# Scores by even and odd query blocks over three PSUM banks, weighted sums in four 64 by 64 tiles, from the third batch on

## The chip, the cores and the metric

The kernel runs on one NeuronCore of a Trainium2 chip. The metric is the device time of one execution in microseconds (us). Three runs of the kernel before gave 892.37, 891.59 and 891.19 us.

## The reference

Masked attention of 8 batches, 8 heads, 576 positions and 64 dimensions feeds a two-layer network with a softplus.

```python
scores = scale * np.matmul(q, k.transpose(0, 1, 3, 2))
mask_local = (rel >= 0) & (rel < stride)
mask_strided = (rel >= 0) & (pos[None, :] % stride == pos[:, None] % stride)
masks = np.stack([mask_local if h < H // 2 else mask_strided for h in range(H)], axis=0)
scores = np.where(masks[None, :, :, :], scores, -1000000000.0)
...
attn = attn / (np.sum(attn, axis=-1, keepdims=True) + 1e-09)
return np.matmul(attn, v).astype(np.float32)
...
h = x @ w_in
g = np.maximum(h, 0.0) + np.log1p(np.exp(-np.abs(h)))
return (g @ w_out).astype(np.float32)
```

The stride is 32, `x` is the attention's output as 4608 tokens of 512, and the layers are 512 by 2048 and 2048 by 512. Four heads look at the last 32 positions (local), four at the positions of their own class modulo 32 (strided). After the host has put the strided heads' positions in the order of their classes, in both kinds a block of 32 queries needs only its own 32 keys and the 32 keys ahead of them.

## The kernel before

**Two heads are a pair**: head 0 lies on partitions 0 to 63 and head 1 on 64 to 127. There are 8 batches times 4 pairs, numbered n = 0 to 31, a local and a strided pair in turn. A pair has 18 blocks of 32 queries, 9 in each half (`place`) of the sequence.

**Scores** of a pair (`score_steps`, L306, matmul in L343) are 36 small matmuls: 18 blocks times two heads, each with 64 rows (dimensions), 32 stationary columns (queries) and 64 moving columns (keys). Operands are fp32, which the chip works off in two passes, so the trace has two rows for each. The 9 blocks of a half are cut into two parts (`SPLIT`): six go to the bank `ps`, three to the upper part of the bank `po`. The two heads take different row halves of the array, and the halves of the sequence and the heads take different column quarters; part 0 takes four of the eight 64 by 32 tiles, and part 1 (`place_of`) the other four. `zip_longest` in `scores` (L353) deals the matmuls of the two parts in turn, as long as both have some.

**Between scores and sums** VectorE adds the mask on the way out of PSUM (`add_mask`, L409; tasks Y), takes maxima, subtracts, sums and normalizes; ScalarE does the exponential; VectorE transposes the weights in blocks of 32 by 32 into `pt` (L451, tasks P).

**Weighted sums** (`weighted`, L502, matmul in L519) use spans of 96 queries: 6 spans times 2 heads are 12 matmuls of 128 rows (the span's 96 keys and the 32 ahead), 64 stationary columns (the values) and 96 moving columns. The two heads are two 128 by 64 tiles. The three spans of half 0 go to the lower part of `po`, those of half 1 to a bank of the pool `ps_h`, named `pv`. From there ScalarE and VectorE make the high and the low part of x (`x_part`, L557 and L555; tasks H and L).

**The network** takes x in chunks of 512 tokens: 16 steps f for each of 9 chunks. A step is `hidden` (L623, tasks F: 12 matmuls of 128 by 128 by 512 into a bank of `ps_h`), the softplus on ScalarE (L635, L638, L640) and VectorE (L644, tasks u), its high and low part (L253 `gh`, L656 `gl`), and two steps later `output` (L663, tasks O: 12 matmuls of the same size into the four banks `py`).

**PSUM has eight banks**: `ps`, `po`, two of `ps_h`, four `py`. The two of `ps_h` are dealt in turn to the steps F and, between them, to `pv`.

**The order of the work** is written out by hand (`FIRST`, L36) up to the first steps of chunk 1; from there the class `Plan` (L80) places tasks with given costs, due times and predecessors on the engines, and the instructions are issued in the order of its start times. From batch 2 on (n = 8 to 31) the scores of pair n and the sums of pair n-1 are one task S{n} on TensorE (L863), placed between an F and an O. The step F after it waits for `L{n-1}1` (L814), the low part of x that is the last reader of `pv`. Pair 8 has no sums ahead of it, and the sums of pair 31 are a task by themselves (L895), so there are 23 such joint tasks.

Of the kernel before, what the change touches and what calls it, by code (L numbers as in the profile page):

```python
# [19 lines left out]
P = 128  # L20
# [99 lines left out]
def attention_softplus_ffn(  # L120
# [32 lines left out]
    st_pool = ctx.enter_context(tc.tile_pool(name="st", bufs=4))  # L153
    u_pool = ctx.enter_context(tc.tile_pool(name="u", bufs=2))
    io_pool = ctx.enter_context(tc.tile_pool(name="io", bufs=4))
    ps_s = ctx.enter_context(tc.tile_pool(name="ps_s", bufs=1, space=bass.MemoryType.PSUM))
    ps_o = ctx.enter_context(tc.tile_pool(name="ps_o", bufs=1, space=bass.MemoryType.PSUM))
    ps_h = ctx.enter_context(tc.tile_pool(name="ps_h", bufs=2, space=bass.MemoryType.PSUM))
# [35 lines left out]

    prob_early = [early["l", pair][:, PAD + S :] for pair in PAIRS[:-1]] + [prob_all]
    prob_early = [t[:, : PAD + 3 * PAD * NCHK] for t in prob_early]
    py = [ps_y.tile([P, DM], F32, name=f"py{t}") for t in range(TPC)]
    ident_b = const.tile([P, P], BF16, name="ident_b")

# [12 lines left out]
    vs, pss, sts, pos, shared = ({} for _ in range(5))  # L212
    taken = []
    phs, us, ghs, gls = {}, {}, {}, {}

    def is_local(n):
        return order[n][1] < NPAIR // 2
# [46 lines left out]
    def load_v(n):  # L264
        b, pair = order[n]
        if n < NPAIR:

            t = room[n]
        else:
            t = v_in  # L270
        t = t[:, : 2 * NTILE * D].rearrange("p (a c) -> p a c", c=2 * D)
        src = v[b, pair]
        nc.sync.dma_start(t[PAD:P, 0], src[0:TILE])  # L273
# [17 lines left out]
    for t in room + [v_in]:  # L291
        nc.gpsimd.memset(t[0:PAD, : 2 * D], 0.0)
# [13 lines left out]
    def score_steps(n, part):  # L306
# [43 lines left out]
        if masked and n == 0:  # L350
            add(False)

    def scores(n, parts=range(2)):  # L353

        for _ in zip_longest(*[score_steps(n, part) for part in parts]):
            pass

    def parts(n, part=None):
        if n not in sts:
            sts[n] = st_pool.tile([P, 4, NCHK], F32, tag="stat", name=f"st_{n}")  # L360
        lo, hi = (0, NCHK) if part is None else SPLIT[part]
# [76 lines left out]
    def normalize(n, engine):  # L438
        pv, _, (_, _, _, rc) = parts(n)
        engine.tensor_tensor(pv, pv, rc.unsqueeze(2).broadcast_to(pv.shape), op=ALU.mult)  # L440

    def prob_transposes(n, quarters=range(4)):
        p = prob_of(n)
        for quarter in quarters:
# [54 lines left out]
        dst = pt_of(n, 2 * g)  # L499
        copy_on(engine, dst, src)  # L500

    def weighted(n, half, joint=False):  # L502


        if joint:
            if half == 0:
                po = shared[n + 1]
            else:
                po = ps_h.tile([P, 512], F32, tag="ph", name=f"pv_{n}")
        elif half == 1 and (n == NPAIR - 1 or n >= 2 * NPAIR):  # L510
            taken.append(n)
            po = ps_s.tile([P, 512], F32, tag="ps", name=f"pv_{n}_{half}")
        else:
            po = ps_o.tile([P, 512], F32, tag="po", name=f"pv_{n}_{half}")
        pos[n, half] = po
        for x in range(NTILE // 2):
            a = NTILE // 2 * half + x
            for h in range(2):
                nc.tensor.matmul(  # L519
                    po[64 * h : 64 * h + 64, TILE * x : TILE * x + TILE],  # L520
                    lhsT=vs[n][:, a, h, :],
                    rhs=pt_of(n, a)[:, h, a % 2],
                    start=True,
                    stop=True,
                )
# [176 lines left out]

    first["mask"] = lambda: nc.scalar.dma_start(mask_b, masks)
    first["W"] = lambda: dummies(10)
    for n in range(2 * NPAIR + 2):
# [83 lines left out]
    def joint(i):  # L789
        return pair_at.get(i, 0) > 2 * NPAIR  # L790
# [4 lines left out]
    for i in range(NFC, len(steps) + 8):  # L795
        when[i] = t
        if i >= begin:
            w = CH[steps[min(i, len(steps) - 1)][0]] / 384
            t += 4.2 * w + (1.3 if i in pair_at else 0) + (1.3 if joint(i) else 0)
    plan = Plan()  # L800
    add = plan.add
    wanted = {}
# [5 lines left out]
    for i in range(begin, len(steps) + LAG):  # L808
        if i < len(steps):
            c, f = steps[i]  # L810
            w, x = CH[c] / 384, when[i]
            after = [f"F{i-1}", f"u{i-2}"] + wanted.get(c, [])
            if joint(i - 1):
                after.append(f"L{pair_at[i - 1] - 1}1")  # L814
            add(f"F{i}", x, "PE", 2.1 * w, lambda c=c, f=f: hidden(c, f), after)
            after = [f"F{i}", f"l{i-2}"]
            add(f"A{i}", x + 2, "ACT", 1.5 * w, lambda c=c, f=f: log_part(c, f), after)
# [27 lines left out]
                fn = lambda c=c, t=t, engine=engine: result(c, t, engine)  # L845
                add(f"y{k}.{t}", x + 0.7 * t + 0.7, e, cost, fn, [name])
    def sums_of(n):
        for half in range(2):
            weighted(n, half, n != last)

    i_of = {n: i for i, n in pair_at.items()}
    for i, n in pair_at.items():
        x = when[i]
        if n > 2 * NPAIR:
            z = x - (when[i] - when[i - 2] if i - 2 in when else 0.0)
            add(f"Q{n}", z, "ACT", 2.5, lambda n=n: lay_out_q(n), [f"q{n}", f"S{n-1}"])
        after = [f"Q{n}", f"k{n}", f"Y{n-1}0", f"Y{n-1}1", f"L{n-2}1"]
        cost = 1.3
        if joint(i):
            cost = 2.5  # L860
            after += [f"P{n-1}", f"v{n-1}", f"u{i-1}"]

        def work(i=i, n=n):  # L863
            scores(n)
# [5 lines left out]
        for j in range(2):  # L870
            after = [f"S{n}", f"P{n-2}"]
            add(f"Y{n}{j}", y + j, "DVE", 0.47, lambda n=n, j=j: add_mask(n, j), after)
        after = [f"Y{n}0", f"Y{n}1"]
        for j, (letter, e, cost, fn) in enumerate(
            (
                ("x", "DVE", 0.75, row_maxima),
# [113 lines left out]
```

## Time and profile before

| What | Value |
|---|---|
| Median of three runs | 891.59 us |
| The profiled execution itself | 891.65 us |
| Span of its trace, first to last instruction | 889.8 us |
| TensorE (PE) busy | 880.2 us, 99% |
| VectorE (DVE) busy | 574.1 us, 65% |
| ScalarE (ACT) busy | 404.7 us, 45% |
| GpSimd (POOL) busy | 56.1 us, 6% |
| DMA, mean over the span | 66 GB/s |

A row of the timeline has the start in us from the span's start, the length in us, the engine, the line of the kernel, the operation, output and inputs, shapes, and how many instructions were merged (x12). PE is the matmul, PEld the load of its stationary operand. Matmuls overlap in their pipeline, so what one costs is read from the distance of two starts and not from its length. In brackets stands how long the engine was idle before, and what released it.

### The profile page before, as it was taken

The page shows a single profiled execution, that of the slowest core. Times are in us where ns is not written, and L with a number is a line of the kernel's source. Part 1 is how long each engine was busy: PE and PEld are TensorE (multiplying, and loading weights), DVE is VectorE, ACT ScalarE, POOL GpSimd, SP SyncE. Part 2 cuts the span into 40 slices and gives each one's busy share as a digit, 9 for nine tenths or more (in the row PEclk, how much of TensorE's full clock was granted, in tenths as well). Part 3 has the DMA queues.
Part 4 walks back from the last instruction along what each step waited for, and adds up shares of the span by engine and source line. Part 5 has one row for each costly group of instructions (what it writes and reads, how often), then busy time and mean ns, then how long its engine had stood idle before and what let it go on. Part 6 is the DMA issues. An engine that isn't in the chain of part 4 may idle for free.

```text
span 889.8 us, 16585 instructions
## 1 busy us (share of the span) xinstructions
PE 880.2 (99%) x6786; PEld 720.1 (81%) x6786; DVE 574.1 (65%) x1263; ACT 404.7 (45%) x764; POOL 56.1 (6%) x84
## 2 busy tenths in 40 slices
PE   8899999999999999999999999999999999999998
PEld 6777888888888888888888888888888888888886
DVE  5878876778766777776766676677777333333332
ACT  5898655354443344344444344334433333333332
POOL 3354340000000000000000000000000000000000
PEclk9999999999999999999999999999999999999999
DMA  9856212222211112111211121111200010001001
GB/s 338 289 200 242 76 34 75 59 60 60 88 32 31 45 54 82 45 31 45 91 45 45 44 92 30 30 43 54 82 18 18 1 48 1 0 1 48 1 1 47
DMA packets 50091, 58.41 MB, mean 66 GB/s; under 512 B 3168, under 2 KB 35296, under 8 KB 50016
## 3 DMA queue, kind: packets, MB, share of 16 engines
q1 hardware_dynamic: 49728, 57.03, 19.9%
q8 instruction: 53, 0.87, 0.4%
q10 hardware_dynamic: 288, 0.33, 0.1%
q14 instruction: 22, 0.18, 0.1%
HBM read 47.91 MB, written 9.44 MB: 64 GB/s over the span
## 4 chain that ended last, share of the span: by engine, by line
PE 96%; DMA 1%; SPq 1%; ACT 0%; DVE 0%; issue 0%; ACTq 0%
PE py L663 45%; PE ph L623 44%; PE ps L343 3%; PE pv L519 2%; PE po L519 2%; DMA early_l<-in_qk_dram 1%; DMA ri<-in_moe_w_in_dram 1%; PE po L343 0%; SPq L273 0%; SPq L262 0%; SPq L563 0%; PE ps L324 0%; SPq L280 0%; SPq L250 0%; PE pt L489 0%
## 5 line engine op out<-in xcount | busy, mean ns | idle before, releaser
L663 PE MATMUL py<-w_o,gh 128*128 128x512 f32 x1152 | 358.4, 392 | 0.0
L623 PE MATMUL ph<-x_h,w_i 128*128 128x512 f32 x1152 | 355.6, 390 | 0.0
L635 ACT ACTIVATE u<-ph 128x512 f32<-128x512 f32 x144 | 86.2, 599 | 399.8 <-PE ph L623 399.5
L623 PEld LDWEIGHTS ph<-x_h,w_i 128*128 128x128 f32 x1152 | 215.7, 188 | 45.3 <-issue 0.2
L663 PEld LDWEIGHTS py<-w_o,gh 128*128 128x128 f32 x1152 | 213.9, 188 | 46.6
L663 PE MATMUL py<-w_o,gl 128*128 128x512 f32 x576 | 224.4, 390 | 0.0
L623 PE MATMUL ph<-x_l,w_i 128*128 128x512 f32 x576 | 224.1, 389 | 0.0
L644 DVE SCALAR_TENSOR_TENSOR u<-ph,u 128x512 f32<-128x512 f32 x144 | 99.3, 690 | 173.2 <-ACT u L640 171.5
L451 DVE STREAM_TRANSPOSE pt<-prob 32x192 f32<-32x192 f32 x448 | 140.1, 317 | 6.8
L663 PEld LDWEIGHTS py<-w_o,gl 128*128 128x128 f32 x576 | 108.1, 188 | 22.8
L623 PEld LDWEIGHTS ph<-x_l,w_i 128*128 128x128 f32 x576 | 108.2, 188 | 22.6
L656 DVE TENSOR_TENSOR gl<-u,gh 128x512 fp32r<-128x512 f32 x136 | 94.3, 694 | 12.0 <-ACT gh L253 1.4
L638 ACT ACTIVATE u<-u 128x512 f32<-128x512 f32 x144 | 91.3, 634 | 4.4
L640 ACT ACTIVATE u<-u 128x512 f32<-128x512 f32 x144 | 91.1, 633 | 4.5
L253 DVE CAST gh<-u 128x512 fp32r<-128x512 f32 x128 | 54.5, 426 | 10.5 <-DVE u L644 0.5
L409 DVE TENSOR_TENSOR prob<-ps,mask_b 128x384 f32<-128x384 f32 x24 | 13.4, 558 | 51.4 <-PE ps L343 51.4
L253 ACT COPY qT<-prob 128x576 f32<-128x576 f32 x28 | 35.9, 1283 | 0.5 <-DMA prob<-in_qk_dram 0.5
L424 ACT ACTIVATE prob<-prob 128x576 f32<-128x576 f32 x24 | 16.5, 687 | 39.3 <-DVE prob L418 39.3
L343 PEld LDWEIGHTS ps<-kT,qT 64*32 64x32 f32 x1440 | 24.8, 106 | 9.7 <-issue 9.3
L343 PE MATMUL ps<-kT,qT 64*32 64x64 f32 x1440 | 30.0, 221 | 0.0
L555 DVE TENSOR_TENSOR x_l<-pv,x_h 128x288 fp32r<-128x288 f32 (+2 forms) x47 | 18.8, 413 | 10.1 <-ACT x_h L557 9.5
L557 ACT CAST x_h<-pv 128x288 fp32r<-128x288 f32 (+2 forms) x47 | 16.8, 375 | 12.6 <-PE pv L519 12.4
(94 smaller groups left out, 483.7 us busy)
## 6 DMA issues: line engine op xcount, KB each, us to landing
v_in<-in_v_dram SPq DMA_DIRECT2D x28, 320.0 KB, 3.5
out_dram<-o SPq DMA_DIRECT2D x35, 256.0 KB, 2.1
ri<-in_moe_w_in_dram SPq DMA_DIRECT2D x16, 512.0 KB, 6.4
ro<-in_moe_w_out_dram SPq DMA_DIRECT2D x16, 512.0 KB, 6.9
kT<-in_qk_dram SPq DMA_DIRECT2D x28, 288.0 KB, 3.3
prob<-in_qk_dram SPq DMA_DIRECT2D x28, 288.0 KB, 2.7
v_in<-in_v_dram SPq DMA_DIRECT2D x28, 48.0 KB, 3.1
room<-in_v_dram SPq DMA_DIRECT2D x4, 320.0 KB, 6.4
```

What stands on the lines that cost most here:

```text
L253: (engine.copy if engine is nc.scalar else engine.tensor_copy)(dst, src)
L343: nc.tensor.matmul(ps[to : to + 32, 64 * (x - lo) : 64 * (x - lo) + 64], lhsT=queries(n, head, c // 32), rhs=k_of(n)[head, c : c + 64], st ...
L451: nc.vector.transpose(pt[32 * (i + c) : 32 * (i + c) + 32, h, a : a + hi - lo, 32 * i : 32 * i + 32,], src[:, lo:hi, 32 * c : 32 * c + 32],)
L519: nc.tensor.matmul(po[64 * h : 64 * h + 64, TILE * x : TILE * x + TILE], lhsT=vs[n][:, a, h, :], rhs=pt_of(n, a)[:, h, a % 2], start=True, ...
L555: nc.vector.tensor_tensor(place("l"), cut(lo, hi), high, op=ALU.subtract)
L623: nc.tensor.matmul(ph, lhsT=w32["i", f][:, half, cc * P : (cc + 1) * P], rhs=x_of(x, cc)[:, t0 : t0 + n], start=(i == 0), stop=(i == 3 * N ...
L635: nc.scalar.activation(us[c, f], phs[c, f], AF.Abs)
L638: nc.scalar.activation(u, u, AF.Exp, scale=-1.0)
L640: nc.scalar.activation(u, u, AF.Ln, bias=1.0)
L644: nc.vector.scalar_tensor_tensor(u, in0=phs.pop((c, f)), scalar=0.0, in1=u, op0=ALU.max, op1=ALU.add)
L656: engine.tensor_tensor(g, us.pop((c, f)), ghs[c, f].bitcast(F32), op=ALU.subtract)
L663: nc.tensor.matmul(py[t], lhsT=g[:, sl], rhs=w32["o", f][:, half], start=(f == 0 and n == 0), stop=(f == NFC - 1 and n == 2),)
```

## The change

For n = 8 and above (`is_late`) three things are done in another way.

**Scores** (`late_scores`): the 9 blocks of a half are dealt by even (five) and odd (four). The even ones go to a bank of `ps_h` (columns 0 to 319), the first three odd ones to `ps` (columns 288 to 479), the fourth odd one to `po` (columns 288 to 351). The matmuls are of the same number and size; even and odd groups of four alternate, and the even blocks take the four tiles of the old part 0, the odd ones the other four. The mask is added in three instructions in place of two, of 320, 192 and 64 columns, with a second mask tile `mask_s` for strided pairs that is loaded by 10 DMAs (`Km`).

**Weighted sums** (`late_weighted`): the keys of a half are cut into five windows of 64. Half 0 lies on partitions 0 to 63 and half 1 on 64 to 127, so half and head make four tiles of 64 by 64. An even block has all its 64 keys in one window; an odd block has 32 in each of two windows, whose sums are added up in PSUM, the other halves of its weights being zeros that four GpSimd memsets write once (`Kz`). A window serves three blocks (96 moving columns), the first and the last two (64): 20 matmuls in place of 12, half 0 into `ps` and half 1 into `po`. The weights' transposes (`late_transposes`) are as many as before, with 160 and 128 columns in place of 192 and 96. The values come in three DMAs for each pair in place of two.

**The plan**: S costs 1.1 and 2.0 in place of 1.3 and 2.5, the times `when` follow, the F after S waits for `Y{n}0` (the mask of the even blocks) in place of `L{n-1}1`, and S waits for `u{i-1}` from n = 8 on.

```diff
+SPLIT_LATE = [(0, 5), (5, 8), (8, 9)]
...
-A15 L70 V71 H71 lo13 Bo14 do14 ho14 lo14 O13 Ae15 L71 v8 Al15 u15 Gh15 Q1 Gh14 Gl14 O14 Bo15
-do15 D8 Q0 QA1 Gl15 Qu1 QA0 Qu0 ho15 lo15 O15 Qh0 y0 Ob15 q9 y1 Qh1 Ql0 y2 y3 Ql1
+A15 L70 V71 Kz H71 lo13 Bo14 do14 ho14 lo14 O13 Ae15 L71 v8 Al15 u15 Gh15 Q1 Gh14 Gl14 O14 Bo15
+do15 D8 Q0 QA1 Gl15 Qu1 QA0 Qu0 ho15 lo15 O15 Qh0 y0 Ob15 q9 Km y1 Qh1 Ql0 y2 y3 Ql1
...
+        pss[n, 0] = ps_h.tile([P, 512], F32, tag="ph", name=f"ps_{n}_0")
+        for j in range(2):
+            pss[n, 1 + j] = shared[n][j][:, S // 2 :]
+        for x in range(5):
+            for part, j, block in ((1, x, 2 * x + 1), (0, x, 2 * x)):
+                if part == 1 and x == 4:
+                    continue
+                if part == 1 and x == 3:
+                    part, j = 2, 0
+                for place in range(2):
+                    c = 9 * 32 * place + 32 * block
+                    for h in range(2):
+                        to = 64 * place + 32 * (h if part == 0 else 1 - h)
...
+        for w in range(5):
+            lo, hi = max(2 * w - 1, 0), min(2 * w + 2, 9)
+            for half in range(2):
+                rows = slice(64 * half, 64 * half + 64)
+                for h in range(2):
+                    nc.tensor.matmul(
+                        banks[half][64 * h : 64 * h + 64, 32 * lo : 32 * hi],
+                        lhsT=vs[n][rows, w, h, :],
+                        rhs=pt_late[rows, h, w, 32 * (lo + 1 - 2 * w) : 32 * (hi + 1 - 2 * w)],
+                        start=w == 0,
+                        stop=w == 4,
...
-            if joint(i - 1):
-                after.append(f"L{pair_at[i - 1] - 1}1")
+            if i - 1 in pair_at:
+                after.append(f"Y{pair_at[i - 1]}0")
...
-        after = [f"Q{n}", f"k{n}", f"Y{n-1}0", f"Y{n-1}1", f"L{n-2}1"]
-        cost = 1.3
+        after = [f"Q{n}", f"k{n}", f"Y{n-1}1", f"Y{n-1}2", f"L{n-2}1"]
+        cost = 1.1
+        after.append(f"u{i-1}")
         if joint(i):
-            cost = 2.5
-            after += [f"P{n-1}", f"v{n-1}", f"u{i-1}"]
+            cost = 2.0
+            after += [f"P{n-1}", f"v{n-1}"]
```

**TensorE, the first joint task** (the scores of pair 9 with the sums of pair 8). Before; `ph` is the hidden step ahead of it, `ps_0` and `po` take the two parts of the scores, `pv` the sums of half 1:

```order
L623 MATMUL ph_5_2061<-x_l_666,w_i_905 128x512
L343 MATMUL ps_0_2080<-kT_101,qT 32x64 x4
L343 MATMUL po_2081<-kT_101,qT 32x64 x4
L343 MATMUL ps_0_2080<-kT_101,qT 32x64 x4
L343 MATMUL po_2081<-kT_101,qT 32x64 x4
L343 MATMUL ps_0_2080<-kT_101,qT 32x64 x4
L343 MATMUL po_2081<-kT_101,qT 32x64 x4
L343 MATMUL ps_0_2080<-kT_101,qT 32x64 x12
L519 MATMUL po_2081<-pt,v_in 64x96 x6
L519 MATMUL pv_2124<-pt,v_in 64x96 x6
L663 MATMUL py_104<-w_o_970,gh_3_2029 128x512 x2
```

And now; `ps_0` is the bank of `ps_h` with the even blocks, `ps` has odd blocks and half 0 of the sums, `po` the last odd block and half 1 of the sums:

```order
L428 MATMUL ps_2099<-kT_104,qT 32x64 x4
L428 MATMUL ps_0_2101<-kT_104,qT 32x64 x4
L428 MATMUL ps_2099<-kT_104,qT 32x64 x4
L428 MATMUL ps_0_2101<-kT_104,qT 32x64 x4
L428 MATMUL ps_2099<-kT_104,qT 32x64 x4
L428 MATMUL ps_0_2101<-kT_104,qT 32x64 x4
L428 MATMUL po_2100<-kT_104,qT 32x64 x4
L428 MATMUL ps_0_2101<-kT_104,qT 32x64 x8
L445 MATMUL ps_2099<-pt,v_in 64x64 x2
L445 MATMUL po_2100<-pt,v_in 64x64 x2
L445 MATMUL ps_2099<-pt,v_in 64x96 x2
L445 MATMUL po_2100<-pt,v_in 64x96 x2
```

Four more rows of 64x96 and two of 64x64 follow, in the same turn of `ps` and `po`, and then the same O as before. The groups of four score matmuls now alternate up to the last two, and the sums alternate between the banks in twos where one bank came after the other in sixes. The places of F, O and S against each other are the same in both programs from batch 2 on.

**VectorE after the same task.** Before; L409 adds the mask, L555 makes the low part of x, L414 takes the maxima:

```order
L409 TENSOR_TENSOR prob<-ps_0_2080,mask_b 128x384
L409 TENSOR_TENSOR prob<-po_2081,mask_b 128x192
L555 TENSOR_TENSOR x_l_376<-po_2081,x_h_362 128x288
L414 TENSOR_REDUCE st_2148<-prob 128x9
L555 TENSOR_TENSOR x_l_376<-pv_2124,x_h_362 128x96
L555 TENSOR_TENSOR x_l_376<-pv_2124,x_h_362 128x192
```

And now, where the same three are L510, L672 and L515:

```order
L510 TENSOR_TENSOR prob<-ps_0_2101,mask_s 128x320
L510 TENSOR_TENSOR prob<-ps_2099,mask_s 128x192
L672 TENSOR_TENSOR x_l_380<-ps_2099,x_h_366 128x288
L510 TENSOR_TENSOR prob<-po_2100,mask_s 128x64
L515 TENSOR_REDUCE st_2177<-prob 128x9
L672 TENSOR_TENSOR x_l_380<-po_2100,x_h_366 128x96
L672 TENSOR_TENSOR x_l_380<-po_2100,x_h_366 128x192
```

One mask instruction has come in between, and it stands ahead of the maxima, of the low part of half 1 and of the softplus (L644, now L761) that follows them.

**GpSimd, late in the part written by hand.** Before; L253 makes the high part of a weight block, L609 the low part:

```order
L253 CAST w_i_1742<-a_i_1570 128x512
L609 TENSOR_TENSOR w_i_1742<-a_i_1570,w_i_1742 128x512
L253 CAST w_o_1762<-a_o_1745 128x512
L253 CAST w_o_1792<-a_o_1748 128x512
L609 TENSOR_TENSOR w_o_1792<-a_o_1748,w_o_1792 128x512
```

And now, with the same two as L263 and L726:

```order
L263 CAST w_i_1746<-a_i_1574 128x512
L726 TENSOR_TENSOR w_i_1746<-a_i_1574,w_i_1746 128x512
L263 CAST w_o_1766<-a_o_1749 128x512
L340 MEMSET pt 32x2x4x32 x4
L263 CAST w_o_1800<-a_o_1752 128x512
L726 TENSOR_TENSOR w_o_1800<-a_o_1752,w_o_1800 128x512
```

The four memsets stand between the two weight blocks, and they wait for the last sums of batch 1.

More of the change, by code (lines that the diff above doesn't have):

```diff
@@ L155, in attention_softplus_ffn @@
     io_pool = ctx.enter_context(tc.tile_pool(name="io", bufs=4))
+    late_pool = ctx.enter_context(tc.tile_pool(name="late", bufs=1))
     ps_s = ctx.enter_context(tc.tile_pool(name="ps_s", bufs=1, space=bass.MemoryType.PSUM))
@@ L272, in load_v @@
         src = v[b, pair]
+        if is_late(n):
+            for half, window in ((0, 0), (0, 1), (1, 0)):
+                key = S // 2 * half - PAD + 64 * window
+                lo = PAD if key < 0 else 0
+                rows = src[key + lo : key + 64]
+                count = 1 if key < 0 else 5 - window
+                step = [64 * 2 * D, count]
+                rows = bass.AP(
+                    tensor=rows.tensor,
+                    offset=rows.offset,
+                    ap=[rows.ap[0], step, rows.ap[1]],
+                )
+                to = t[64 * half + lo : 64 * half + 64, window : window + count]
+                nc.sync.dma_start(to, rows)
+            vs[n] = t.rearrange("p a (h d) -> p a h d", d=D)
+            return
         nc.sync.dma_start(t[PAD:P, 0], src[0:TILE])
@@ L292, in attention_softplus_ffn, with late_masks, late_zeros @@
         nc.gpsimd.memset(t[0:PAD, : 2 * D], 0.0)
+    def late_masks():
+        for first, rows, homes, to in (
+            (6, (0, 64), ((0, 64), (64, P)), (0, 6)),
+            (6, (64, P), ((0, 64), (64, P)), (1, 7)),
+            (9, (0, P), ((0, P),), (5, 2)),
+        ):
+            src = masks[rows[0] : rows[1], 64 * first : 64 * first + 3 * 64]
+            src = src.rearrange("p (a c) -> p a c", c=64)
+            for lo, hi in homes:
+                dst = mask_s[lo:hi].rearrange("p (a c) -> p a c", c=64)
+                nc.sync.dma_start(dst[:, to[0] : to[0] + 4 : 3], src[:, 0:3:2])
+                nc.sync.dma_start(dst[:, to[1]], src[:, 1])
+    def late_zeros():
+        for half in range(2):
+            for c, windows, cols in ((1, slice(1, 5), slice(0, 32)), (0, slice(0, 4), slice(64, 96))):
+                rows = slice(64 * half + 32 * c, 64 * half + 32 * c + 32)
+                nc.gpsimd.memset(pt_late[rows, :, windows, cols], 0.0)
     def mask_of(n, part):
+        if is_late(n):
+            if is_local(n):
+                return mask_b[:, (0, 64, 64)[part] : (5 * 64, 4 * 64, 2 * 64)[part]]
+            return mask_s[:, 64 * SPLIT_LATE[part][0] : 64 * SPLIT_LATE[part][1]]
         if is_local(n):
@@ L351, in score_steps, with late_banks, late_scores, late_weighted @@
             add(False)
+    def late_banks(n):
+        shared[n] = (
+            ps_s.tile([P, 512], F32, tag="ps", name=f"ps_{n}"),
+            ps_o.tile([P, 512], F32, tag="po", name=f"po_{n}"),
+        )
+    def late_scores(n):
+        pss[n, 0] = ps_h.tile([P, 512], F32, tag="ph", name=f"ps_{n}_0")
[11 more added lines that the diff above has]
+                        to = 64 * place + 32 * (h if part == 0 else 1 - h)
+                        head = slice(64 * h, 64 * h + 64)
+                        nc.tensor.matmul(
+                            pss[n, part][to : to + 32, 64 * j : 64 * j + 64],
+                            lhsT=queries(n, head, c // 32),
+                            rhs=k_of(n)[head, c : c + 64],
+                            start=True,
+                            stop=True,
+                        )
+    def late_weighted(n, banks):
+        for half in range(2):
+            pos[n, half] = banks[half]
+        for w in range(5):
+            lo, hi = max(2 * w - 1, 0), min(2 * w + 2, 9)
+            for half in range(2):
+                rows = slice(64 * half, 64 * half + 64)
+                for h in range(2):
+                    nc.tensor.matmul(
+                        banks[half][64 * h : 64 * h + 64, 32 * lo : 32 * hi],
[3 more added lines that the diff above has]
+                        stop=w == 4,
+                        skip_group_check=True,
+                    )
     def scores(n, parts=range(2)):
@@ L360, in parts @@
             sts[n] = st_pool.tile([P, 4, NCHK], F32, tag="stat", name=f"st_{n}")
[L361 removed]
+        lo, hi = (0, NCHK) if part is None else (SPLIT_LATE if is_late(n) else SPLIT)[part]
         sv = None
@@ L440, in normalize, with late_transposes @@
         engine.tensor_tensor(pv, pv, rc.unsqueeze(2).broadcast_to(pv.shape), op=ALU.mult)
+    def late_transposes(n, quarter):
+        p = prob_of(n)
+        half, h = divmod(quarter, 2)
+        even = p[64 * half + 32 * h :][:32, 0:5]
+        odd = p[64 * half + 32 * (1 - h) :][:32, 5:9]
+        for src, c, kb, windows, col in (
+            (even, 0, 0, slice(0, 5), 32),
+            (even, 1, 1, slice(0, 5), 32),
+            (odd, 0, 1, slice(0, 4), 64),
+            (odd, 1, 0, slice(1, 5), 0),
+        ):
+            lo = 64 * half + 32 * kb
+            nc.vector.transpose(
+                pt_late[lo : lo + 32, h, windows, col : col + 32],
+                src[:, :, 32 * c : 32 * c + 32],
+            )
     def prob_transposes(n, quarters=range(4)):
         p = prob_of(n)
+        if is_late(n):
+            for quarter in quarters:
+                late_transposes(n, quarter)
+            return
         for quarter in quarters:
@@ L500, in early_copy, with weighted @@
         copy_on(engine, dst, src)
[L502 to L510, printed above, removed]
+    def weighted(n, half):
+        if half == 1 and n == NPAIR - 1:
             taken.append(n)
@@ L704, in attention_softplus_ffn @@
     first["W"] = lambda: dummies(10)
+    task("Km", late_masks)
+    task("Kz", late_zeros)
     for n in range(2 * NPAIR + 2):
@@ L847, in sums_of @@
     def sums_of(n):
-        for half in range(2):
-            weighted(n, half, n != last)
+        if n == last:
+            late_banks(n + 1)
+        late_weighted(n, shared[n + 1])
     i_of = {n: i for i, n in pair_at.items()}
@@ L869, in attention_softplus_ffn @@
         y = x + 1.5
-        for j in range(2):
+        for j in range(3):
             after = [f"S{n}", f"P{n-2}"]
             add(f"Y{n}{j}", y + j, "DVE", 0.47, lambda n=n, j=j: add_mask(n, j), after)
-        after = [f"Y{n}0", f"Y{n}1"]
+        after = [f"Y{n}0", f"Y{n}1", f"Y{n}2"]
         for j, (letter, e, cost, fn) in enumerate(
```

11 lines of the change are left out of this document (9 added, 2 removed).

## The prediction

> **What bounds the kernel now.** I read the page first, its busy times and the chain that ended last, and then the list of what TensorE waited for.
>
> ```profile
> span 889.8 us, 16585 instructions
> ...
> PE 880.2 (99%) x6786; PEld 720.1 (81%) x6786; DVE 574.1 (65%) x1263; ACT 404.7 (45%) x764; POOL 56.1 (6%) x84
> ...
> PE 96%; DMA 1%; SPq 1%; ACT 0%; DVE 0%; issue 0%; ACTq 0%
> ```
>
> ```profile
> PE py L343 <- issue: 1.6, 1, 1.6
> PE idle L686 <- DVE room L205: 1.2, 1, 1.2
> PE pv L519 <- DVE st L378: 1.2, 1, 1.2
> ...
> PE pt L489 <- POOL early_l L440: 0.4, 1, 0.4
> PE py L324 <- ACT early_l L392: 0.3, 1, 0.3
> ```
>
> The columns of the second view are total us, times and the longest. TensorE is the chain, and these few waits are all on tiles of the first 32 us. After that it never stands still for another engine. So the change is worth what it takes off TensorE's own rows, unless it makes a new wait. Next come the rows of TensorE around one joint task, here the one at 407 us.
>
> ```profile
> 407.44 0.39 PE L623 MATMUL ph<-x_l,w_i 128*128 128x512 f32 x1
> 407.76 0.26 PE L343 MATMUL ps<-kT,qT 64*32 64x64 f32 x4
> 407.78 0.26 PE L343 MATMUL po<-kT,qT 64*32 64x64 f32 x4
> 407.84 0.24 PE L343 MATMUL ps<-kT,qT 64*32 64x64 f32 x4
> 407.86 0.24 PE L343 MATMUL po<-kT,qT 64*32 64x64 f32 x4
> 407.89 0.24 PE L343 MATMUL ps<-kT,qT 64*32 64x64 f32 x4
> ...
> 407.95 0.24 PE L343 MATMUL ps<-kT,qT 64*32 64x64 f32 x4
> ...
> 408.28 0.49 PE L343 MATMUL ps<-kT,qT 64*32 64x64 f32 x20
> 408.70 0.72 PE L519 MATMUL po<-pt,v_in 128*64 128x96 f32 x12
> 409.25 0.67 PE L519 MATMUL pv<-pt,v_in 128*64 128x96 f32 x12
> 409.84 0.73 PE L663 MATMUL py<-w_o,gh 128*128 128x512 f32 x2
> 410.41 0.40 PE L663 MATMUL py<-w_o,gl 128*128 128x512 f32 x1
> ...
> 412.70 0.62 PE L623 MATMUL ph<-x_h,w_i 128*128 128x512 f32 x2
> ...
> 415.42 0.62 PE L663 MATMUL py<-w_o,gh 128*128 128x512 f32 x2
> ...
> 418.14 0.62 PE L623 MATMUL ph<-x_h,w_i 128*128 128x512 f32 x2
> ```
>
> A hidden step of 12 matmuls takes 415.42 - 412.70 = 2.72, so 0.227 for one. The last one starts at 407.44 and the first output at 409.84, 2.40 later where 0.23 would do: 2.17 go to the task, and 0.12 more to the two slow starts behind it (0.57 from 409.84 to 410.41 for two, in place of 0.45). That is 2.29 us, 23 times, 53 us of the span. The first and the last of the 23 take as long:
>
> ```profile
> 158.95 0.39 PE L623 MATMUL ph<-x_l,w_i 128*128 128x512 f32 x1
> 161.36 0.73 PE L663 MATMUL py<-w_o,gh 128*128 128x512 f32 x2
> 672.25 0.39 PE L623 MATMUL ph<-x_l,w_i 128*128 128x512 f32 x1
> 674.65 0.73 PE L663 MATMUL py<-w_o,gh 128*128 128x512 f32 x2
> ```
>
> **Weighted sums.** The last two passes of the sums, from a narrow window of the timeline:
>
> ```profile
> 409.66 0.25 PE L519 MATMUL pv<-pt,v_in 128*64 128x96 f32 x2
> ```
>
> The second half of the sums starts at 409.25, its last two passes at 409.66: its 12 passes go in six rounds of two (the two heads side by side), and a round of 96 columns takes 0.41 / 5 = 0.083. The first half took 409.25 - 408.70 = 0.55, 0.05 more than six rounds, which I put down to the first load of weights of a new shape. From the last round to the output it is 0.18, a round and 0.10 for the change of shape. Together 12 x 0.083 + 0.05 + 0.10 = 1.14, as the rows have it (408.70 to 409.84).
>
> What a round of 64 columns on 64 rows takes, the scores show: from 407.84 to 407.95 there are two rounds, 0.055 each, and in each run eight passes, both heads (rows 0 to 63 and 64 to 127) on all four column quarters. So row halves and column parts of the array do run side by side here, into two banks at a time, and the four 64 by 64 tiles should as well. The new sums then are ten rounds of four passes, two for each window: 4 x 0.055 (first and last window) + 6 x 0.083 = 0.72. With the 0.05 and the 0.10, and 0.01 for two tiles more to start, this makes 0.88. **Gain 0.26 in each of 23 tasks**, and as much in the sums of pair 31 that stand alone. Bounds: 0.15 if a round is never under 0.083, as no row shows a 64 column round with weights of 64 columns; 0.31 if the 0.05 is not paid. I take 0.26, since the scores' rounds and the sums' rounds both go with their columns.
>
> The Trainium skill has a rule against this ("TensorE: Matmul & The Clock Gate", the section "Wait — 56ns, not 53.3ns?"): starts of matmuls are never closer than about 25 ns, however small they are. By that the 40 new passes would take at least 1.0 us, no less than the 24 old ones. The trace does not agree: 72 passes of scores start within 0.8 us.
>
> **Scores.** As many passes of the same shape. Eight tiles are in use only while groups of four from both parts alternate. Before, three groups in a row end on `ps`; the row of 20 passes at 408.28 is this stretch, on four tiles alone. Now only the last two groups share their tiles. One group less in the longest chain on the same tiles is two rounds, 0.11, at most; but the mixed stretch ahead (from 408.02 to 408.28) goes slower than the burst at the start, so the group that moves into it costs something there. Gain between 0 and 0.11; I take the middle, 0.05, and also once for pair 8's scores.
>
> **Sum.** 23 x (0.26 + 0.05) = 7.1, + 0.26 + 0.05 = 7.4 us. The profiled execution took 891.65 us, 1.9 over its span and 0.06 over the median. 891.65 - 7.4 = **884.3 us**.
>
> **What I cost at nothing, and its cover.** VectorE's and ScalarE's rows after the same task:
>
> ```profile
> 404.39 0.69 DVE L644 SCALAR_TENSOR_TENSOR u<-ph,u 128x512 f32<-128x512 f32 x1 [3.03 <-ACT u L640]
> ...
> 408.81 0.56 DVE L409 TENSOR_TENSOR prob<-ps,mask_b 128x384 f32<-128x384 f32 x1 [2.40 <-PE ps L343]
> 410.10 0.36 DVE L409 TENSOR_TENSOR prob<-po,mask_b 128x192 f32<-128x192 f32 x1 [0.74 <-ACT x_h L557]
> ...
> 411.40 0.45 DVE L555 TENSOR_TENSOR x_l<-pv,x_h 128x288 fp32r<-128x288 f32 x1
> 411.76 0.68 DVE L644 SCALAR_TENSOR_TENSOR u<-ph,u 128x512 f32<-128x512 f32 x1
> ...
> 413.48 0.69 DVE L656 TENSOR_TENSOR gl<-u,gh 128x512 fp32r<-128x512 f32 x1
> ```
>
> A mask instruction takes 0.56 for 384 columns and 0.36 for 192, so 0.16 whatever its size: the third one puts 0.16 at most ahead of the maxima, x's low part, the softplus and the parts of g. The softplus then ends at 412.6; its bank is wanted by the F at 418.14, 0.31 earlier now, 5.2 us on. The low part of g ends at 414.3 and is used by the output behind that F. The F after the task used to wait for the low part of x (ends 411.85, for a start at 412.70); it now waits for the first mask instruction, which ends at 409.37, for a start at 412.39: 3.0 us of slack. The scores' fifth matmul now waits for the softplus that ended at 405.08, 2.7 us ahead of it (before, the first sum into `pv` did). Transposes: as many, and as many columns. If one of these covers went, it would cost 2.3 us for each 0.1 that is then missing.
>
> GpSimd and SyncE, once, before batch 2 (the first two rows are groups with us of all and mean ns of one):
>
> ```profile
> L292 POOL MEMSET room<- 32x128 f32 x4 | 0.6, 194 | 0.0
> L290 POOL MEMSET early_l<- 128x32 f32 x3 | 0.3, 114 | 0.0
> ```
>
> ```profile
> 127.97 1.30 POOL L609 TENSOR_TENSOR w_o<-a_o,w_o 128x512 fp32r<-128x512 f32 x1
> ```
>
> ```profile
> 132.85 0.62 PE L663 MATMUL py<-w_o,gh 128*128 128x512 f32 x2
> ```
>
> ```profile
> 139.81 1.40 SPq L679 DMA_DIRECT2D out_dram<-o  x3
> ```
>
> From 32 to 128 columns a memset grows by 80 ns, so 256 columns are about 0.30 (an estimate), four 1.2. The low part of the weight block behind them then ends near 130.6 in place of 129.27; the output that takes it starts at 132.85. Ten mask DMAs at 0.47 (1.40 / 3) hold SyncE 4.7 us; behind them stand only three results and loads for pair 10. The masks are wanted by pair 9's scores, at 159 us. The third load of values is 0.47 of SyncE in a stretch of 18 us or more, for sums a whole stretch later.
>
> **Rivals.**
>
> *The row halves take turns.* If the two halves of the keys, on partitions 0 to 63 and 64 to 127, could not run together with 64 wide weights, the sums would be 20 rounds of two: 8 x 0.055 + 12 x 0.083 = 1.44 in place of 1.00. Each task would lose 0.44 - 0.05, in all 23 x 0.39 + 0.44 - 0.05 = 9.4: 901.1 us, slower. For it: no row has 64 by 64 tiles. Against it: the scores' rounds of eight. It decides when less than about 0.55 of a half's 0.72 runs beside the other. Chance 0.04.
>
> *The issue of passes binds.* The old sums start their last pass 0.96 after the first (408.70 to 409.66). If each of the 40 new passes took 0.024 to issue, the last would start as late as now, and only the scores' gain would be left: 23 x 0.05 = 1.2 us, 890.4; with the scores held back as well, 891.6, no change. Against it are the 20 passes at 408.28, which start within 0.28, 0.014 each, on half of the tiles. The Trainium skill's floor, named above, would have this come true, and the trace speaks against it. Chance 0.04.
>
> *A new wait.* The F after the task would lose all of the gain only if the first mask instruction came 3.3 us later, or the softplus ahead of the scores 2.7. What speaks for it is only that VectorE's queue has an instruction more. 891.6 us, no change. Chance 0.02.
>
> *The plan's own costs are right.* They fall by 0.2 for a task's scores and 0.4 for its sums. That would be 23 x 0.6 = 13.8 and 878 us. Against it: the sums' rounds go with their columns, so 0.31 is the most they can give. Chance 0.03.
>
> **How the numbers follow.** Chance of the forecast 0.87. A measurement of this kernel tells about 0.2% (1.8 us) from no change. The ends of the unknown costs, all at once, are 23 x 0.15 + 0.15 = 3.6 us (888.0) and 23 x 0.42 + 0.42 = 10.1 us (881.6); the range takes nearly all of that, 881.8 to 887.0, and leaves the rivals out. Faster: 0.87 + 0.03 = 0.90. Same: 0.04 + 0.02 = 0.06. Slower: 0.04.
>
> **What would show it.** From the last hidden matmul ahead of a joint task to the first output after it there should be 2.09 us in place of 2.40, in every one of 23; the sums should start four passes at a time, and ten rounds should last 0.72 from the first start to the end of the last round, besides the 0.05. The list of TensorE's waits should keep its few early rows and get none from F, O or the scores. VectorE should show three mask rows in each task and end its softplus no more than 0.2 later. Wrong it would be if the sums' passes start in twos, 0.04 or more apart on the mean, or if an F after a task has idle time ahead of it.

## The result, and the profile after

The changed kernel took 884.76 us, the median of four runs (884.52 to 885.84), beside 891.98 for the kernel before (four runs: the three named above and one of 895.02), a ratio of 0.9915, 95% interval 0.989 to 0.994. It is faster by 7.2 us; forecast were 7.4 us and 884.3.

The page of the execution after, its span and its busy times:

```profile
span 884.1 us, 17431 instructions
...
PE 871.1 (99%) x7170; PEld 712.5 (81%) x7170; DVE 573.5 (65%) x1287; ACT 405.0 (46%) x764; POOL 57.4 (6%) x88
```

TensorE is still busy for 99% of the span, and its busy time fell by 9 us. What it waited for (total us, times, longest):

```profile
PE pv L636 <- issue: 3.1, 2, 2.9
PE py L395 <- issue: 1.4, 2, 1.0
...
PE pv L636 <- DVE x_l L672: 0.9, 2, 0.5
PE ps L395 <- ACT w_o L263: 0.8, 1, 0.8
PE py L376 <- ACT early_l L493: 0.3, 1, 0.3
```

All waits of this list lie in the first 70 us, in the part of the program that the change doesn't touch; no row is of a hidden step (now L740), an output (L780), late scores (L428) or late sums (L445). So the gain has to lie in TensorE's own rows. Its timeline around the same joint task as was shown of before, with the first hidden matmul after the task in the last row:

```profile
405.63 0.39 PE L740 MATMUL ph<-x_l,w_i 128*128 128x512 f32 x1
405.94 0.67 PE L428 MATMUL ps<-kT,qT 64*32 64x64 f32 x44
406.39 0.24 PE L428 MATMUL po<-kT,qT 64*32 64x64 f32 x1
...
406.41 0.24 PE L428 MATMUL po<-kT,qT 64*32 64x64 f32 x1
...
406.85 0.27 PE L445 MATMUL ps<-pt,v_in 64*64 64x64 f32 x2
406.86 0.27 PE L445 MATMUL po<-pt,v_in 64*64 64x64 f32 x2
406.95 0.23 PE L445 MATMUL ps<-pt,v_in 64*64 64x64 f32 x2
...
407.51 0.22 PE L445 MATMUL ps<-pt,v_in 64*64 64x64 f32 x2
...
407.56 0.22 PE L445 MATMUL ps<-pt,v_in 64*64 64x64 f32 x2
...
407.73 0.73 PE L780 MATMUL py<-w_o,gh 128*128 128x512 f32 x2
408.30 0.40 PE L780 MATMUL py<-w_o,gl 128*128 128x512 f32 x1
...
410.61 0.39 PE L740 MATMUL ph<-x_h,w_i 128*128 128x512 f32 x1
```

From the last hidden matmul to the first output it is 407.73 - 405.63 = 2.10, where it was 2.40. The sums go from 406.85 to 407.73, 0.88 in place of 1.14 (with three decimals 0.887 and 1.141); from the first score to the first sum it is 0.900 in place of 0.944, which the rounded rows blur. Two passes into `ps` and two into `po` start within 0.02, on all four tiles, the next four 0.10 later, and so on for ten rounds. The two slow starts behind the task are as they were (0.57 from 407.73 to 408.30), but the output step as a whole is 0.02 longer: 410.61 - 407.73 = 2.88, where it was 412.70 - 409.84 = 2.86. The first and the last of the 23 take as long:

```profile
160.22 0.39 PE L740 MATMUL ph<-x_l,w_i 128*128 128x512 f32 x1
162.33 0.50 PE L780 MATMUL py<-w_o,gh 128*128 128x512 f32 x1
...
667.35 0.39 PE L740 MATMUL ph<-x_l,w_i 128*128 128x512 f32 x1
669.46 0.50 PE L780 MATMUL py<-w_o,gh 128*128 128x512 f32 x1
```

With three decimals each task is 0.298 shorter (2.403 to 2.105), pair 8's scores alone 0.045, pair 31's sums alone 0.254: 23 x 0.298 + 0.045 + 0.254 = **7.15 us**. Two smaller amounts stand outside this sum: the output step behind each task is 0.018 longer (0.44 us in all), and from the last task's first output to the end of the span it is 191.70 in place of 192.06 (0.36 shorter). They nearly cancel, 7.07 us, and the medians say 7.2.

The profiled execution itself took 885.84 us, 5.8 less than the one of before. The rest was lost ahead of the change: the last hidden matmul ahead of pair 8's scores starts at 142.75 here, and at 141.47 before. The third row below is that place in an execution of another variant (the one with eight tiles), whose work up to there is the same as this kernel's:

```profile
141.47 0.39 PE L623 MATMUL ph<-x_l,w_i 128*128 128x512 f32 x1
```

```profile
142.75 0.39 PE L740 MATMUL ph<-x_l,w_i 128*128 128x512 f32 x1
```

```profile
140.89 0.39 PE L751 MATMUL ph<-x_l,w_i 128*128 128x512 f32 x1
```

Over the eleven profiled executions of this kernel and its variants it lies between 140.89 and 144.23. A single profile therefore can't tell a microsecond, but its joint tasks can tell 0.01 each. The four memsets and ten DMAs that the change adds have no part in these 1.28 us, as the first of them starts at 128.57 (below) and the lag is there by 70 us. The same hidden step, before and after:

```profile
68.74 0.72 PE L623 MATMUL ph<-x_h,w_i 128*128 128x512 f32 x2
```

```profile
70.03 0.73 PE L740 MATMUL ph<-x_h,w_i 128*128 128x512 f32 x2
```

Of this lag 0.8 us are the wait on ScalarE in the list above (`w_o`), which ends at 69.22, and 0.4 us come from the first 32 us.

VectorE after the same task (L510 adds the mask, L761 is the softplus):

```profile
406.95 0.49 DVE L510 TENSOR_TENSOR prob<-ps,mask_b 128x320 f32<-128x320 f32 x1 [2.36 <-PE ps L428]
408.30 0.36 DVE L510 TENSOR_TENSOR prob<-ps,mask_b 128x192 f32<-128x192 f32 x1 [0.85 <-ACT x_h L674]
...
408.94 0.21 DVE L510 TENSOR_TENSOR prob<-po,mask_b 128x64 f32<-128x64 f32 x1
409.18 0.76 DVE L515 TENSOR_REDUCE st<-prob 128x9 f32<-128x576 f32 x1
...
410.22 0.68 DVE L761 SCALAR_TENSOR_TENSOR u<-ph,u 128x512 f32<-128x512 f32 x1
```

There are three mask rows. The first ends at 407.44, 3.2 ahead of the hidden matmul at 410.61 that waits for it.

### The profile page after: what moved, and what is told of

The parts are those of the page before. It is cut to its first block, busy times and chain, and to the rows that moved or that the text cites. A ratio compares the mean times of both kernels' runs of the same rounds, so it can differ in the third digit from the quotient of the medians.

```text
span 884.1 us, 17431 instructions
## 1 busy us (share of the span) xinstructions
PE 871.1 (99%) x7170; PEld 712.5 (81%) x7170; DVE 573.5 (65%) x1287; ACT 405.0 (46%) x764; POOL 57.4 (6%) x88
## 4 chain that ended last, share of the span: by engine, by line
PE 97%; DMA 1%; ACT 1%; issue 1%; DVE 0%; SPq 0%; DVEq 0%; ACTq 0%
PE py L780 45%; PE ph L740 44%; PE ps L428 2%; PE ps L445 2%; PE pv L636 1%; DMA early_l<-in_qk_dram 1%; PE ps L395 1%; PE po L445 0%; PE py L395 0%; PE pt L611 0%; PE po L428 0%; PE ps L376 0%; DVE x_l L672 0%; SPq L260 0%; ACT early_l L263 0%
## 5 line engine op out<-in xcount | busy, mean ns | idle before, releaser
L780 PE MATMUL py<-w_o,gh 128*128 128x512 f32 x1152 | 358.7, 392 | 0.0
L740 PE MATMUL ph<-x_h,w_i 128*128 128x512 f32 x1152 | 355.5, 390 | 0.0
L740 PEld LDWEIGHTS ph<-x_h,w_i 128*128 128x128 f32 x1152 | 215.7, 188 | 45.4 <-issue 0.2
L780 PEld LDWEIGHTS py<-w_o,gh 128*128 128x128 f32 x1152 | 213.9, 188 | 45.6
L780 PE MATMUL py<-w_o,gl 128*128 128x512 f32 x576 | 224.6, 390 | 0.0
L740 PE MATMUL ph<-x_l,w_i 128*128 128x512 f32 x576 | 224.1, 389 | 0.0
L761 DVE SCALAR_TENSOR_TENSOR u<-ph,u 128x512 f32<-128x512 f32 x144 | 99.0, 688 | 176.0 <-ACT u L757 174.3
L780 PEld LDWEIGHTS py<-w_o,gl 128*128 128x128 f32 x576 | 108.1, 188 | 23.1
L740 PEld LDWEIGHTS ph<-x_l,w_i 128*128 128x128 f32 x576 | 108.2, 188 | 22.5
L555 DVE STREAM_TRANSPOSE pt<-prob 32x128 f32<-32x128 f32 (+1 forms) x384 | 119.6, 316 | 6.1
L263 DVE CAST gh<-u 128x512 fp32r<-128x512 f32 x128 | 53.4, 418 | 8.4
L263 ACT COPY qT<-prob 128x576 f32<-128x576 f32 x28 | 35.9, 1281 | 0.2 <-DMA prob<-in_qk_dram 0.2
L510 DVE TENSOR_TENSOR prob<-ps,mask_b 128x320 f32<-128x320 f32 (+1 forms) x24 | 10.1, 424 | 35.7 <-PE ps L428 26.1
L510 DVE TENSOR_TENSOR prob<-ps,mask_s 128x320 f32<-128x320 f32 (+1 forms) x24 | 10.2, 425 | 32.3 <-PE ps L428 22.0
L428 PEld LDWEIGHTS ps<-kT,qT 64*32 64x32 f32 x1536 | 19.4, 105 | 8.5 <-issue 8.5
L428 PE MATMUL ps<-kT,qT 64*32 64x64 f32 x1536 | 23.3, 223 | 0.0
L445 PE MATMUL ps<-pt,v_in 64*64 64x96 f32 (+1 forms) x480 | 22.6, 238 | 0.0
```

The costliest lines, as they stand in the source:

```text
L263: (engine.copy if engine is nc.scalar else engine.tensor_copy)(dst, src)
L428: nc.tensor.matmul(pss[n, part][to : to + 32, 64 * j : 64 * j + 64], lhsT=queries(n, head, c // 32), rhs=k_of(n)[head, c : c + 64], start= ...
L445: nc.tensor.matmul(banks[half][64 * h : 64 * h + 64, 32 * lo : 32 * hi], lhsT=vs[n][rows, w, h, :], rhs=pt_late[rows, h, w, 32 * (lo + 1 - ...
L510: nc.vector.tensor_tensor(pv, sv, m, op=ALU.add)
L555: nc.vector.transpose(pt_late[lo : lo + 32, h, windows, col : col + 32], src[:, :, 32 * c : 32 * c + 32],)
L740: nc.tensor.matmul(ph, lhsT=w32["i", f][:, half, cc * P : (cc + 1) * P], rhs=x_of(x, cc)[:, t0 : t0 + n], start=(i == 0), stop=(i == 3 * N ...
```

## The experiments

My theory: the gain is array time, fewer rounds on the busiest tile, for the sums (0.254 of the 0.298) and for the scores (0.044). Rivals: the spread over three banks makes it; the planner's new costs make it; the issue of matmuls is what binds. Of each kernel I give the time and, from its trace, the joint task from the last hidden matmul to the first output, which all 23 share unless said otherwise.

**The changed kernel again.**

> The changed kernel once more. Every theory: 884.8 us, all 23 joint tasks at 2.105 us from the start of the last hidden matmul to the first output, as in its first profile. If the 1.3 us that its first profile lost before batch 2 are chance of that execution, the scores of the ninth pair (alone) start nearer 141.7 than 143.0 us here, and the profiled execution is near 884.6; if they come from the change, they start near 143.0 again.

It took 885.82 us (six runs, 884.35 to 886.51) beside 892.21, ratio 0.9916 (0.990 to 0.993); all 23 tasks 2.105. The hidden matmul ahead of pair 8 started at 142.37, between the two cases. Here too the lag behind the kernel before, 0.90, stands whole by 70 us (the hidden step shown above starts at 69.63 in place of 68.74). Since the same early work ends as soon as 140.89 in a variant, chance can account for the whole difference.

**Even and odd blocks on the same four tiles.**

```diff
-                        to = 64 * place + 32 * (h if part == 0 else 1 - h)
+                        to = 64 * place + 32 * h
```

The transposes read the odd blocks from the same rows.

> Odd blocks' queries go to the same four tiles of 64 by 32 as the even ones; three banks, sums and plan as in the changed kernel. Array tiles set the time (my theory): each tile takes nine blocks of two passes of 55.8 ns, 1.00 us, where now the last pass starts 0.76 us after the first; the scores take 0.22 to 0.25 us more in each of 24 tasks, 5.3 to 6.0 us: 890.4 us. It is the spread over three banks (rival): 884.8 us as now.

891.15 us (ten runs), ratio 0.998 (0.997 to 0.999): 5.3 over the changed kernel measured beside it. One joint task:

```profile
384.12 0.39 PE L740 MATMUL ph<-x_l,w_i 128*128 128x512 f32 x1
384.44 0.88 PE L428 MATMUL ps<-kT,qT 64*32 64x64 f32 x48
...
385.58 0.27 PE L445 MATMUL ps<-pt,v_in 64*64 64x64 f32 x2
...
386.47 0.50 PE L780 MATMUL py<-w_o,gh 128*128 128x512 f32 x1
```

The scores take 385.58 - 384.44 = 1.14 to the first sum in place of 0.90, the sums 0.89 as in the changed kernel: 2.344, so 24 x 0.239 = 5.7 us. The spread over three banks does not shorten the scores by itself; it takes the second set of tiles.

**The old sums under the new scores.**

```diff
-        for w in range(5):
...
-                        lhsT=vs[n][rows, w, h, :],
...
+        for half in range(2):
+            for x in range(NTILE // 2):
...
+                        lhsT=vs[n][:, a, h, :],
+                        rhs=pt[:, h, a],
```

> The weighted sums as before the change, twelve matmuls of 128 rows by 64 columns over 96 queries, with v and the transposed probabilities laid out for them; scores, banks, waits and plan as changed. Array tiles set the time: twelve rounds of 0.083 in place of ten of 0.72 together, 0.887 becomes 1.14, 0.255 us in each of 24 tasks, 6.1 us: 890.9 us. Banks or plan (rival): 884.8 us. Their VectorE transposes are three times as many and smaller; if those came to bind, PE would show waits of its own in the list of waits and the time would pass 892.

899.22 us (four runs), ratio 1.007 (1.004 to 1.009): 0.7% slower than the kernel before, not 890.9, and past the 892 at which the transposes were to show. 19 joint tasks took the 2.360 of the theory, but the first four, which follow each other most closely, took 3.90 to 4.32, and the list of waits has a new row. The second fence groups the transposes of this kernel, the third those of the changed one (busy us and mean ns of one):

```profile
PE ps L428 <- DVE u L759: 6.1, 4, 1.7
```

```profile
L553 DVE STREAM_TRANSPOSE pt<-prob 32x64 f32<-32x64 f32 (+1 forms) x1152 | 211.1, 205 | 11.7
```

```profile
L555 DVE STREAM_TRANSPOSE pt<-prob 32x128 f32<-32x128 f32 (+1 forms) x384 | 119.6, 316 | 6.1
```

Three times as many transposes, 91 us more on VectorE, and the scores wait for the softplus behind them. This was the cover that the prediction had counted on for the wait on `u`. To separate the two, the same sums with the changed kernel's sixteen transposes:

> The old twelve sums on v laid out as before the change, but with the changed kernel's sixteen VectorE transposes, so that the probabilities do not lie where these sums read them; everything else as changed. If VectorE made the rest of the loss where the transposes were three times as many, PE now waits as little as in the changed kernel, all 23 joint tasks take 2.360 us, and the time is 885.3 + 24 x 0.255 = 891.4 us. If it was not the transposes, near 899 us again.

892.03 us (ten runs), ratio 1.000 (0.999 to 1.001), and all 23 tasks at 2.360:

```profile
384.46 0.39 PE L738 MATMUL ph<-x_l,w_i 128*128 128x512 f32 x1
...
385.68 0.72 PE L444 MATMUL ps<-pt,v_in 128*64 128x96 f32 x12
386.22 0.67 PE L444 MATMUL po<-pt,v_in 128*64 128x96 f32 x12
386.82 0.50 PE L778 MATMUL py<-w_o,gh 128*128 128x512 f32 x1
```

The sums are 1.14 again (386.82 - 385.68), into the new banks. So 0.255 a task is the tiles' alone, and the 7.1 us that the fuller version's four long tasks lost on top were VectorE's.

**The new sums twice.** The call of the twenty sums stands in a loop of two.

> The twenty sums of each late pair issued twice into the same places (the first matmul of each sum starts afresh, so what is computed stays). Array tiles set the time: ten more rounds, 0.72 us in each of 24 tasks, 17.3 us: 902.6 us, and this is the price of the new sums by themselves (the old twelve rounds would be 24.0). Issue alone sets it (rival): 20 matmuls at 16.7 ns, 0.33 us each, 8.0 us: 893.3 us.

903.04 us (four runs), ratio 1.012 (1.010 to 1.014). Each task is 2.833, 0.728 more, as ten rounds: 4 x 0.055 + 6 x 0.083 = 0.72. Issue alone, 20 x 0.0167 = 0.33, would have given half.

**One half of the keys after the other.**

```diff
-        for w in range(5):
-            lo, hi = max(2 * w - 1, 0), min(2 * w + 2, 9)
-            for half in range(2):
-                rows = slice(64 * half, 64 * half + 64)
+        for half in range(2):
+            rows = slice(64 * half, 64 * half + 64)
+            for w in range(5):
+                lo, hi = max(2 * w - 1, 0), min(2 * w + 2, 9)
```

> The twenty sums in another order: ten of the first half of the keys, then ten of the second, where now the halves alternate. Matmuls start in the order of issue and a tile's next one holds up all behind it (my theory): two of four tiles work at a time, twenty rounds in place of ten, 0.72 us more in each of 24 tasks: 902.6 us. The queue lets a matmul of a free tile start ahead of one whose tile is busy (rival): the second half starts after some of the first's, 0 to 0.3 us more: 885 to 892 us.

896.11 us (four runs), ratio 1.004 (1.003 to 1.006), each task 2.602, 0.497 more: between the two, and neither was right. The sums of one task:

```profile
387.13 0.75 PE L445 MATMUL ps<-pt,v_in 64*64 64x64 f32 x14
387.64 0.27 PE L445 MATMUL po<-pt,v_in 64*64 64x64 f32 x2
387.71 0.25 PE L445 MATMUL ps<-pt,v_in 64*64 64x96 f32 x2
...
387.79 0.22 PE L445 MATMUL ps<-pt,v_in 64*64 64x64 f32 x2
...
387.85 0.22 PE L445 MATMUL ps<-pt,v_in 64*64 64x64 f32 x2
...
388.51 0.50 PE L780 MATMUL py<-w_o,gh 128*128 128x512 f32 x1
```

All of `ps` was issued ahead of all of `po`, yet `po` starts at 387.64, ahead of the last three rounds of `ps`. Those are the second pass of the fourth matmul and both of the fifth: one whole matmul of each tile waits beside the running one, and the queue passes it. Then 0.51 + 0.87 = 1.38. The Trainium skill ("TensorE: Matmul & The Clock Gate", the section "The mechanism") says that matmuls start and end strictly in program order; the starts in these rows do not agree.

**All even blocks, then all odd ones.** The loop over odd and even goes outside the loop over blocks.

> The scores in another order: all twenty matmuls of the even blocks, then all sixteen of the odd ones, where now they alternate. If only about one matmul a tile can wait for its tile and holds up all behind it, as the order of the halves showed for the sums (my theory): the odd ones start when the fifth even round is due, after some 0.45 us, and take 0.45 more: 0.90 to 0.95 us in place of 0.754 from the first to the last pass, 24 x 0.17 = 4.1 us, 889.1 us. If a deep queue lets them start at once (rival), 0.754 stays: 885.0 us.

887.77 us in one execution; each task is 2.240, the scores 0.889 from the first pass to the last, just under the theory's range (0.90 to 0.95) and far from the rival's 0.754. The price of the order is 0.135 a task. It is not enough that both sets of tiles are used; neighbours in the order have to go to different ones.

**Four more score matmuls.**

```diff
-                if part == 1 and x == 4:
-                    continue
-                if part == 1 and x == 3:
-                    part, j = 2, 0
+                if part == 1 and x >= 3:
+                    part, j, block = 2, 0, 7
```

> The four score matmuls of the last odd block are issued a second time into the same places, between the last odd and the last even block: the odd tiles then have five blocks, as the even ones have (what is computed stays). If the issue of matmuls sets the scores' time since the change (my theory: of the 36, the later ones start 16.7 ns apart), four more are 0.067 us: scores of 0.821 in place of 0.754 us from the first to the last pass, 24 x 0.067 = 1.6 us, 886.6 us. If the busiest tile still sets it (rival), its five blocks stay five: 0.754 and 885.0 us.

Each task is 2.172, so 0.067 for four, and the scores take 0.82. That this one execution took 890.52 us says little: its start of pair 8 was the latest of all (144.23), and 2.9 us of it lie outside the span, where 1.8 is usual. So four more matmuls on the less busy tiles cost 0.0167 each: the pace at which matmuls are issued bears on the scores' time now, and the busiest tile alone does not set it. It can be seen in the changed kernel's own rows: single passes into `po` at 406.39 and 406.41. "Issue" is a name for this pace; whether it is the issuing itself or the loading of the stationary operands, of which every pass has one (7170 of each on the page), no run separates.

**The sums on eight tiles.**

```diff
-                for h in range(2):
+                for s in range(4):
+                    h, d = s // 2, 32 * (s % 2)
...
-                        banks[half][64 * h : 64 * h + 64, 32 * lo : 32 * hi],
-                        lhsT=vs[n][rows, w, h, :],
+                        pos[n, half][s][32 * s : 32 * s + 32, 32 * lo : 32 * hi],
+                        lhsT=vs[n][rows, w, h, d : d + 32],
```

> The sums in eight tiles of 64 by 32, the same shape as the scores' tiles, forty matmuls in place of twenty, each tile still ten passes of 0.72 us together; the fourth odd block goes to the even blocks' tiles, and the sums of a half lie in alternate banks by quarters of 32 rows, so that x is taken out by four instructions in place of one. Array tiles and their change of shape set the time: the change of shape between scores and sums (about 0.09 us) goes, so does 0.025 of a longer first load, 0.115 us in 24 tasks, 2.8 us: 882.0 us; if sums start on the tiles that the scores leave early, up to 0.2 us each: 880.0. The issue of matmuls binds (rival): 20 matmuls more at 16.7 ns are 0.33 us, less what was saved, 5.2 us: 890.0 us.

970.14 us (four runs), ratio 1.086 (1.083 to 1.088). Even an undisturbed task got longer, 2.192; its scores take 0.844 from the first pass to the last in place of 0.754, as the fourth odd block is on the even blocks' tiles. Its sums and the output, then a wait of its list, then one of the eight instructions each that make the high and the low part of x (L685, L683):

```profile
423.12 0.24 PE L446 MATMUL ps<-pt,v_in 64*32 64x64 f32 x1
...
424.10 0.22 PE L446 MATMUL po<-pt,v_in 64*32 64x64 f32 x1
424.25 0.50 PE L791 MATMUL py<-w_o,gh 128*128 128x512 f32 x1
```

```profile
PE ph L751 <- DVE u L772: 46.6, 59, 2.0
```

```profile
427.64 0.45 DVE L683 TENSOR_TENSOR x_l<-po,x_h 32x288 fp32r<-32x288 f32 x1
```

The change of shape did go: sums start on free tiles (423.12) while scores still run (up to 423.22). But forty matmuls then take 424.10 - 423.12 = 0.98, more than the 0.72 of a tile's ten rounds; in pair 31, where no scores run beside them, they still take 0.87 (from 772.37 to 773.24). What sets this pace isn't settled. The large loss is elsewhere: 32 partitions take VectorE 0.45 us, as long as 128 did in the kernel before (the row at 411.40), so x costs four times as much, and the softplus and the hidden step behind it come late. The forecast had named the four instructions and given them no cost.

**The old costs of the planner.**

```diff
-            t += 4.2 * w + (1.1 if i in pair_at else 0) + (0.9 if joint(i) else 0)
+            t += 4.2 * w + (1.3 if i in pair_at else 0) + (1.3 if joint(i) else 0)
```

The task's own costs are 1.3 and 2.5 again.

> The changed kernel with the planner's costs of before (1.3 and 1.3 us a pair in the sum of due times, 1.3 and 2.5 us for the task). My theory: PE runs from task to task without a wait in either order, so 885.3 us, within 0.9. The plan's costs made part of the gain (rival): 891 us.

885.02 us (four runs), ratio 0.992 (0.990 to 0.994), all 23 tasks 2.105. The planner's costs make none of the gain.

No variant beat the changed kernel.

## Why the prediction was right, and where it was not

- **The bound.** TensorE without waits after the early part, so that a gain is worth only what leaves its rows: held, in both profiles. That the medians came so close to the 7.4 (7.2 us) is in part luck: when the same two kernels were measured again for the control, they differed by 6.4.
- **Weighted sums, 0.26 forecast.** 0.254 in the rows, and 0.255 when the old sums come back by themselves. The parts hold too: ten rounds, 0.728 when doubled, and 0.05 more in the first round (0.10 from 406.85 to 406.95, where a later one of 64 columns, 407.51 to 407.56, takes 0.05).
- **Scores, 0.05 forecast, as the middle of 0 and 0.11.** 0.044 to 0.045. The upper end came from rounds on the busiest tile. Nine blocks on each of four tiles do cost 0.24 more; but with the blocks dealt five to four, the busiest tile alone no longer sets the time, as four more matmuls on the others cost 0.067. The prediction saw that a mixed stretch goes slower and could not say why; a pace of 0.0167 for a matmul fits a gain that stopped short. That half of the bound was so nearly right is luck. Nor is the whole of the 0.754 accounted for: 36 x 0.0167 is 0.60, and five blocks on a tile are 10 x 0.056 = 0.56.
- **Row halves take turns (rival, 901.1).** They don't: four tiles start within 0.02. Even with the halves issued one after the other it was 896.1, as the queue passes one waiting matmul of each tile.
- **Issue binds (rival, about 890 to 892).** Wrong for the 20 sums, by the doubled sums. For the scores it holds in part: each further matmul costs 17 ns. Forty sums on eight tiles also take longer than their tiles need.
- **The plan's costs (rival, 878), a new wait (rival, 891.6).** Neither: the old costs give the same time, and no wait appeared. The second is a matter of cover, though: the variant with small transposes and the one with eight tiles show how it comes about, by VectorE's queue.
- **The output step, put at nothing.** The prediction gave the matmuls behind the task no change; the step is 0.018 longer, 0.44 us in all. Why isn't shown; it is not the new sums as such, as the stretch from one late task's output to the next task, 21.67 before and 21.69 now, is 21.71 under the old sums with sixteen transposes and 21.67 with the new sums twice.
- **Work off the path, mis-sized without effect.** The softplus ends 410.90 - 405.63 = 5.27 after the last hidden matmul; before, 412.44 - 407.44 = 5.00. That is 0.27, not "no more than 0.2". The step that failed is the 0.16 for the third mask instruction: 64 columns were taken as moved from the first one, but that one is over long before VectorE waits for x's high part, so they are an addition behind that wait (409.18 - 408.94 = 0.24). The four memsets took 1.33, not 1.2. A mask DMA took 0.60 of SyncE, not 0.47, ten of them 7.0 us, not 4.7. Of GpSimd the rows show the memsets and, behind them, the low part of the weight block; of SyncE the first mask DMA and the results behind the last:

```profile
128.57 1.33 POOL L340 MEMSET pt<- 32x256 f32 x4 [1.93 <-PE pv L636]
...
130.67 1.30 POOL L726 TENSOR_TENSOR w_o<-a_o,w_o 128x512 fp32r<-128x512 f32 x1
```

```profile
141.06 0.60 SPq L332 DMA_DIRECT2D mask_s<-in_masks_dram  x1
...
148.07 1.34 SPq L796 DMA_DIRECT2D out_dram<-o  x3
```

TensorE waited for none of them: no row of its waits names them.

## What to carry to other kernels

When TensorE never waits, count what the busiest part of its array does in a stretch, in rounds of so many columns, and beside it how many matmuls are issued at 0.017 us each. The larger of the two is the least that the stretch takes: it was the time of the 20 sums (0.72), but the scores took 0.754 where the counts give 0.56 and 0.60, and forty sums took 0.87 to 0.98 where they give 0.72 and 0.67. Deal small matmuls so that neighbours in the order go to different tiles, as in these runs the queue passed no more than one waiting matmul a tile. Before cutting tiles further, count the instructions of the other engines that have to follow: 32 partitions took VectorE 0.45 us, and so did 128.

## What was not expected of the hardware

- Matmuls of different tiles start out of the order of issue: sums on `po` 0.07 to 0.21 us ahead of earlier ones on `ps` (387.64 against 387.71 to 387.85), and on eight tiles sums ahead of scores (423.12, scores up to 423.22).
- Behind a first burst, small score matmuls start one in 0.0167 us, and four more cost four times that (0.067).
- From the output of one late task to the next task the same matmuls take 21.67 us in one program and up to 21.71 in another, with no wait in either.
- The part of the program ahead of pair 8 ends anywhere in a range of 3.3 us from one execution to the next, while the joint tasks repeat to 0.001 us.
